# Reading the two halves of a matmul's moving operand in turn

## The chip, the cores and the metric

The kernel runs on one core of a Trainium2 chip. The metric is the device time of one execution in microseconds. Three runs of the kernel before gave 926.76, 927.38 and 1300.62 us; their median is 927.38 us.

## The reference

The inputs are `q`, `k`, `v` of shape 8 x 8 x 576 x 64 (batch, heads, sequence, head width) and three weight matrices. `k` and `v` are averaged over groups of 8 positions, so each head has 72 keys. Attention with softmax over these keys gives `x` of 4608 tokens x 512. A gated feed-forward block follows:

```python
gate = 1.0 / (1.0 + np.exp(-(x @ w_gate)))      # 4608x512 @ 512x1536
val = x @ w_val                                  # 4608x512 @ 512x1536
return (gate * val @ w_out).astype(np.float32)   # 4608x1536 @ 1536x512
```

Everything is float32. The three products of the feed-forward block (gate, value, output) are nearly all of the arithmetic.

## The kernel before, in words

The 4608 tokens are cut into 9 blocks of 512 (`BT`). Block 0 is done in a first pass (`first_pass`), with plain products. The other eight blocks are done as four pairs, and each of the three products of a pair is done with Strassen's seven products (numbered 1 to 7 as `m`) on halves of the matrices.

To keep float32 accuracy, each operand is split in two float32r parts, high and low (`split`), and each product is the sum of three matmuls: high x high, high x low, low x high. One TensorE matmul has a stationary operand of 128x128 (`lhsT`), which a weight load brings into the array, and a moving operand of 128 rows x 512 columns (`rhs`), which is streamed through it. The result, 128x512 float32, is summed up in a PSUM bank. In the names of the trace, `chain<-xo,parts` is a matmul of the gate and value products with `xo` (the activations, 512 tokens) moving and `parts` (weights) stationary, in `product` and `whole`. `acc<-hs,oparts` is a matmul of the output product in `second_sums`, with `hs` (the gated activations, 512 tokens) moving. `acc<-oparts,hs` is one of the output product of block 0 in `accumulate`, where the output weights `oparts` move (512 output columns) and `hs` is stationary.

In SBUF each moving operand is a contiguous run of 512 float32 words in each of the 128 partitions, and the matmul reads it from the first word to the last. Only the last step of the last pair splits one matmul group in a left and a right half of 256 columns.

Attention of the coming pair, the weight preparation (conversion of weights, the Strassen sums, splits), the activations and the stores run on DVE, ACT, POOL and the DMA queues beside the matmuls. The order of all instructions on every engine is fixed by hand: `ORDER` lists the work of the first pass word by word, `LATER` is a list of unit numbers for the four pairs. Line 320, on which the trace puts every instruction, is the one line through which recorded instructions are issued, so instructions are told apart by their tiles.

Block 0 leaves the kernel as rows (`out`, 512 tokens x 512), the other blocks transposed (`outT`, 512 x 4096), and the host puts both together.

Of the kernel before, what the change touches and what calls it, by code (L numbers as in the profile page):

```python
# [19 lines left out]
P = 128  # L20
# [6 lines left out]
DM, DF = 512, 1536  # L27
NC = DM // P
NF = DF // P
BT = 512  # L30
NB = B * S // BT
# [241 lines left out]
"""  # L273


class Taken:
# [56 lines left out]
def attention_then_ffn(ctx: ExitStack, tc: tile.TileContext, qT, kT, vm, vr, vn, sums8, wgv, wo, const, out, outT):  # L333
# [48 lines left out]
    words, parts, plain, oparts, wholes = {}, {}, {}, {}, {}  # L382
# [170 lines left out]
    def reload_s(m, q):  # L553

        t = otile([P, 2, 2, HALF], F32R, "oparts")
        if m < 4:
            half = slice(HALF, DM) if m == 3 else slice(0, HALF)
            for k in range(2):
                f = 4 * q + 2 * k + (m > 1)
                nc.sync.dma_start(t[:, k].bitcast(F32), kept_o[f][:, :, half].bitcast(F32))  # L560
        else:
            nc.sync.dma_start(t.rearrange("p k h n -> p k (h n)").bitcast(F32), kept_s[m, q].bitcast(F32))
        oparts[m, q] = t
# [254 lines left out]
    def product(kind, p, m):  # L818

        b = {1: "A", 6: "A", 7: "A", 4: "A", 2: "B", 5: "C", 3: "C"}[m]  # L820
        if m in (1, 2, 5):
            bank[kind, b] = ps.tile([P, BT], F32, name="chain", tag=CHAIN["GV".index(kind) * 3 + "ABC".index(b)])
        t, w, x = bank[kind, b], parts.pop((kind, p, m)), xo[m]
        with book.unit():
            for c in range(NC // 2):
                a = slice(c * P, (c + 1) * P)
                for k, (h, y) in enumerate(((0, 0), (0, 1), (1, 0))):
                    nc.tensor.matmul(
                        t, lhsT=w[:, h, a], rhs=x[:, y, c],
                        start=(m in (1, 2, 5) and c == 0 and k == 0), stop=(c == 1 and k == 2), skip_group_check=True,  # L830
                    )
        if m in (1, 5, 6):
            s = snap.tile([P, BT], F32, name=f"s{kind}{m}")
            nc.scalar.copy(s, t)
            seen[kind, m] = s
            return
        q = {2: (0, 0), 3: (0, 1), 7: (1, 1), 4: (1, 0)}[m]
        if m != 4:
            y = two.tile([P, BT], F32, name="y", tag="y")
            nc.vector.tensor_tensor(out=y, in0=t, in1=seen[kind, {2: 1, 3: 6, 7: 5}[m]], op=ALU.add)  # L840
        else:
            y = t
        if kind == "G":
            if m in (2, 7):
                gates[q[0]] = snap.tile([P, 2, BT], F32, name=f"gate{q[0]}")
            nc.scalar.activation(gates[q[0]][:, q[1]], y, AF.Sigmoid)
        else:
            f = 2 * p + q[1]
            nc.vector.tensor_tensor(
                out=hb[f // 4][:, f % 4, q[0] * BT:(q[0] + 1) * BT], in0=y, in1=gates[q[0]][:, q[1]], op=ALU.mult  # L850
            )
# [7 lines left out]
    def whole(kind, f, side, t=None):  # L859

        if t is None:
            t = ps.tile([P, BT], F32, name="chain", tag=CHAIN[turn[0] % 6])
            turn[0] += 1
        w = plain[kind, f]
        for c in range(NC):
            a = slice(c % 2 * P, c % 2 * P + P)
            x = xo[((1, 2), (5, 4))[side][c // 2]]
            with book.unit():
                for k, (h, y) in enumerate(((0, 0), (0, 1), (1, 0))):
                    nc.tensor.matmul(  # L870
                        t, lhsT=w[:, c // 2, h, a], rhs=x[:, y, c % 2],
                        start=(c == 0 and k == 0), stop=(c == NC - 1 and k == 2),
                    )
            yield t
# [139 lines left out]
    def second_sums(n, last, build, later):  # L1014
        A, B_, C = ("b4", "b5"), ("b0", "b3"), ("b1", "b2")
        acc, seen2 = {}, {}

        def result(side, half, c, bank, add):

            if add is None:  # L1020
                t = snap.tile([P, BT], F32, name="o", tag=f"sV{5 + c}")
            else:
                t = two.tile([P, BT], F32, name="o", tag="y")
            r, a = (half * 2 + c) * P, (2 * n - 2 + side) * BT
            if add is None and last and c:
                for k, copy in enumerate((nc.scalar.copy, nc.vector.tensor_copy)):
                    z = slice(k * BT // 2, (k + 1) * BT // 2)
                    copy(t[:, z], bank[:, z])
                    nc.sync.dma_start(outT[r:r + P, a + z.start:a + z.stop], t[:, z])
                return  # L1030
            if add is None:
                nc.scalar.copy(t, bank)
            else:
                nc.vector.tensor_tensor(out=t, in0=bank, in1=add, op=ALU.add)
            nc.sync.dma_start(outT[r:r + P, a:a + BT], t)

        units = [(m, q) for m in ((1, 5, 6, 2, 7, 3, 4) if last else (1, 5, 6, 2, 3, 7, 4)) for q in qs[n]]
        for u in units[:2]:
            reload_s(*u)
        for i, (m, q) in enumerate(units):  # L1040
            if i + 2 < len(units):
                reload_s(*units[i + 2])
            if i == 1:
                first_sums(qs[n][2])
            if i + 2 < len(units):
                operand(i + 2, *units[i + 2], n)
            hs = halves.pop((m, q))
            w = oparts.pop((m, q))
            name = {1: "A", 6: "A", 7: "A", 4: "A", 2: "B", 5: "C", 3: "C"}[m]
            cols, left, right = (slice(0, BT),), (slice(0, BT // 2),), (slice(BT // 2, BT),)  # L1050
            steps = ((0, (0, 1), cols), (1, (0, 1), cols))
            if last and i + 1 == len(units):
                steps = ((0, (0,), cols), (1, (0,), cols), (0, (1,), cols), (1, (1,), left), (1, (1,), right))
            for k, cs, (z,) in steps:
                with book.unit():
                    for c in cs:
                        if i % 3 == 0 and k == 0 and m in (1, 2, 5):
                            acc[name, c] = ps.tile([P, BT], F32, name="acc", tag={"A": A, "B": B_, "C": C}[name][c])
                        for t, (h, y) in enumerate(((0, 0), (0, 1), (1, 0))):
                            nc.tensor.matmul(  # L1060
                                acc[name, c][:, z], lhsT=w[:, k, h, c * P:(c + 1) * P], rhs=hs[:, y, k, z],
                                start=(m in (1, 2, 5) and i % 3 == 0 and k == 0 and t == 0), stop=(i % 3 == 2 and k == 1 and t == 2),
                                skip_group_check=True,
                            )
                if i == 0 and k == 1:
                    product("V", TURNS[n][-1], 4)
                    consumed("V", TURNS[n][-1], 4)
            if i % 3 == 2:
                for c in range(2):
                    t = acc[name, c]  # L1070
                    if m in (1, 5, 6):
                        s = snap.tile([P, BT], F32, name=f"s{'GV'[c]}{m}")
                        nc.scalar.copy(s, t)
                        seen2[m, c] = s
                    else:
                        side, half = {2: (0, 0), 3: (0, 1), 7: (1, 1), 4: (1, 0)}[m]
                        result(side, half, c, t, None if m == 4 else seen2[{2: 1, 3: 6, 7: 5}[m], c])
            if i in (8, 10, 12, 14, 19, 20):
                next(build, None)
        for _ in build:  # L1080
            pass
        for _ in range(3):
            next(later, None)
        s1.clear()
# [8 lines left out]
    def first_pass():  # L1093
# [46 lines left out]
        scs, rests, av, vp, raws, conv, ygate, vbank, hss, acc, outs, turned = ({} for _ in range(12))  # L1140
# [222 lines left out]
        def accumulate(f):  # L1363
            for i in range(QT):
                if f == 0:
                    acc[i] = bank_for([P, DM], "acc")
                a = slice(i * P, (i + 1) * P)
                for k, (y, w) in enumerate(((0, 0), (1, 0), (0, 1))):
                    nc.tensor.matmul(
                        acc[i], lhsT=hss[f // 2][:, y, f % 2, a], rhs=oparts[f // 2][:, f % 2, w],  # L1370
                        start=(f == 0 and k == 0), stop=(f == NF - 1 and k == 2),
                    )

# [90 lines left out]
```

## Time and profile before

| | |
|---|---|
| median of three runs | 927.38 us |
| span of the profiled execution | 924.9 us, 12542 instructions |
| PE (matmuls) busy | 914.2 us, 99% |
| PEld (weight loads) busy | 758.0 us, 82% |
| DVE busy | 694.2 us, 75% |
| ACT busy | 572.9 us, 62% |
| POOL busy | 24.1 us, 3% |
| DMA | 223.13 MB, mean 241 GB/s |
| granted TensorE clock | 0.998 of full speed, mean |

The profiled execution has no time of its own beside its span: the span is counted from the first to the last instruction, and the median of the runs shown is 2.5 us above it. PE and PEld are two rows for one engine, TensorE: weight loads run beside matmuls. Matmuls are pipelined, so the duration of one (about 390 ns for 512 columns) is longer than its share of the engine's time; the pace is read from the distance between the starts of matmuls that follow each other.

### The profile page before, as it was taken

The numbers are of one execution on the slowest core, as the hardware profiler recorded it, in microseconds if no ns is written. First come the engines' busy times: TensorE is split into PE (matmuls) and PEld (weight loads), VectorE is DVE, ScalarE is ACT, GpSimd is POOL, SyncE is SP. The second block draws the span as 40 slices with busy tenths as digits, with TensorE's granted clock in tenths as the row PEclk, the third lists the DMA queues.
The fourth block names the chain that finished last, engine by engine and source line by source line (L and its number), as shares of the span: only waits on it lengthen the run. The fifth ranks groups of instructions, "written<-read, shape, count | busy, mean of one in ns | idle before, by whom it ended". The sixth has DMA issues, their size and how long they took to land.

```text
span 924.9 us, 12542 instructions
## 1 busy us (share of the span) xinstructions
PE 914.2 (99%) x4375; PEld 758.0 (82%) x4375; DVE 694.2 (75%) x1062; ACT 572.9 (62%) x1044; POOL 24.1 (3%) x59
## 2 busy tenths in 40 slices
PE   8999999999999999999999999999999999999998
PEld 7778888888888888888888888888888888888886
DVE  6999978899999997886779966454668744444763
ACT  6999998689989665655466637343454443324442
POOL 1000000012120000000000000000000000000000
PEclk9999999999999999999999999999999999999999
DMA  9998786778989768897666676555556776555366
GB/s 332 378 359 323 281 308 248 274 238 297 327 301 329 256 193 261 291 308 231 211 216 223 198 236 229 180 166 178 181 174 196 229 223 222 176 193 182 97 208 197
DMA packets 90367, 223.13 MB, mean 241 GB/s; under 512 B 9536, under 2 KB 28480, under 8 KB 88768
## 3 DMA queue, kind: packets, MB, share of 16 engines
q1 hardware_dynamic: 85184, 203.97, 66.0%
q0 software_dynamic: 5120, 18.35, 5.0%
q8 instruction: 35, 0.57, 0.3%
q14 instruction: 28, 0.23, 0.1%
HBM read 168.81 MB, written 53.48 MB: 240 GB/s over the span
## 4 chain that ended last, share of the span: by engine, by line
PE 89%; ACT 5%; DVE 3%; DMA 1%; issue 1%; SPq 0%; DVEq 0%; ACTq 0%
PE chain L320 53%; PE acc L320 27%; PE av L320 4%; PE sc L320 4%; PE tp L320 2%; DMA early<-in_qT 1%; ACT L320 1%; DMA raw<-in_vr 1%; ACT parts L320 1%; ACT e L320 1%; SPq L320 0%; DVE early L320 0%; ACT early L320 0%; ACT raw L320 0%; DVE zs L320 0%
## 5 line engine op out<-in xcount | busy, mean ns | idle before, releaser
L320 PE MATMUL chain<-xo,parts 128*128 128x512 f32 x2316 | 559.7, 394 | 0.8 <-DVE y L320 0.8
L320 PEld LDWEIGHTS chain<-xo,parts 128*128 128x128 f32 x2316 | 427.5, 188 | 88.7 <-DVE y L320 1.4
L320 PE MATMUL acc<-hs,oparts 128*128 128x512 f32 x1011 | 235.3, 390 | 0.1
L320 PEld LDWEIGHTS acc<-hs,oparts 128*128 128x128 f32 x1011 | 188.2, 188 | 39.5 <-issue 1.0
L320 ACT CAST hs<-h 128x1024 fp32r<-128x1024 f32 x52 | 54.8, 1054 | 55.3 <-PE acc L320 48.0
L320 DVE TENSOR_TENSOR hs<-h,hs 128x1024 fp32r<-128x1024 f32 x52 | 63.4, 1221 | 32.4 <-ACT hs L320 32.4
L320 DVE TENSOR_TENSOR y<-chain,sV 128x512 f32<-128x512 f32 x69 | 47.3, 687 | 46.5 <-PE chain L320 28.2
L320 DVE TENSOR_TENSOR y<-chain,sG 128x512 f32<-128x512 f32 x69 | 47.1, 687 | 42.8 <-PE chain L320 25.6
L320 ACT COPY sV<-chain 128x512 f32<-128x512 f32 x69 | 40.3, 586 | 57.5 <-PE chain L320 50.1
L320 ACT ACTIVATE gate<-y 128x512 f32<-128x512 f32 x69 | 43.1, 632 | 43.7 <-DVE y L320 41.3
L320 ACT COPY sG<-chain 128x512 f32<-128x512 f32 x69 | 40.1, 587 | 47.1 <-PE chain L320 46.8
L320 ACT ACT_TABLE_LOAD x47 | 60.3, 1283 | 2.4 <-DVE m L320 1.3
L320 ACT CAST hs<-s 128x1024 fp32r<-128x1024 f32 x36 | 37.9, 1053 | 35.3 <-PE acc L320 23.8
L320 DVE TENSOR_TENSOR h<-y,gate 128x512 f32<-128x512 f32 x69 | 47.3, 689 | 2.0 <-ACT gate L320 0.4
L320 DVE TENSOR_TENSOR hs<-s,hs 128x1024 fp32r<-128x1024 f32 x36 | 43.9, 1220 | 4.4 <-ACT hs L320 4.3
L320 PE MATMUL sc<-kbd,raw 128*128 128x144 f32 (+1 forms) x260 | 41.1, 294 | 0.1
L320 PEld LDWEIGHTS sc<-kbd,raw 128*128 128x128 f32 (+1 forms) x260 | 34.3, 177 | 8.2 <-issue 2.6
L320 PE MATMUL acc<-oparts,hs 128*128 128x512 f32 x144 | 37.8, 398 | 0.0
L320 PEld LDWEIGHTS acc<-oparts,hs 128*128 128x128 f32 x144 | 26.4, 188 | 5.4 <-DVE early L320 0.2
L320 DVE TENSOR_TENSOR h<-h 128x256 f32<-128x256 f32 (+2 forms) x39 | 28.2, 727 | 2.0 <-DMA h<-keptwV 1.5
L320 DVE TENSOR_REDUCE m<-sc 128x4 f32<-128x288 f32 x48 | 21.7, 452 | 10.0 <-PE sc L320 9.7
L320 DVE TENSOR_TENSOR h<-chain,gate 128x512 f32<-128x512 f32 x23 | 15.8, 687 | 14.6 <-PE chain L320 14.6
(195 smaller groups left out, 1028.4 us busy)
## 6 DMA issues: line engine op xcount, KB each, us to landing
oparts<-keptS SPq DMA_DIRECT2D x48, 512.0 KB, 3.7
oparts<-keptO SPq DMA_DIRECT2D x72, 256.0 KB, 3.4
raw<-in_wgv SPq DMA_DIRECT2D x12, 1024.0 KB, 8.1
out<-o SPq DMA_DIRECT2D x35, 256.0 KB, 4.5
raw<-in_kT SPq DMA_DIRECT2D x28, 288.0 KB, 4.8
raw<-in_qT SPq DMA_DIRECT2D x29, 256.0 KB, 4.3
raw_o<-in_wo SPq DMA_DIRECT2D x12, 512.0 KB, 6.3
keptO<-oparts SPq DMA_DIRECT2D x12, 512.0 KB, 4.0
```

The source lines that it names most:

```text
L320: return self._book.take(lambda: f(*args, **named))
```

## The change

A helper `by_halves` turns a run of 512 words into the order 0, 256, 1, 257, 2, 258 and so on. The matmuls of the three products read their moving operand in that order. The number of matmuls, their columns, their stationary operands and their destinations in PSUM are the same; the result's columns come out in the turned order. For the gate and value products the columns are tokens, so `h` and `hs` hold tokens in turned order, and the output product of the pairs turns them a second time. In block 0 the tokens are turned once (by the first two products) and the output columns once (by the third). The host puts rows and columns back in place after the device is done. Matmuls of the attention part, transposes and weight loads are as before.

```diff
+def by_halves(x):
+
+    return x.rearrange("p (i j) -> p j i", i=2)
@@ product
-                        t, lhsT=w[:, h, a], rhs=x[:, y, c],
+                        t, lhsT=w[:, h, a], rhs=by_halves(x[:, y, c]),
@@ whole
-                        t, lhsT=w[:, c // 2, h, a], rhs=x[:, y, c % 2],
+                        t, lhsT=w[:, c // 2, h, a], rhs=by_halves(x[:, y, c % 2]),
@@ second_sums
-                                acc[name, c][:, z], lhsT=w[:, k, h, c * P:(c + 1) * P], rhs=hs[:, y, k, z],
+                                acc[name, c][:, z], lhsT=w[:, k, h, c * P:(c + 1) * P],
+                                rhs=by_halves(hs[:, y, k])[:, z.start // 2:z.stop // 2],
@@ accumulate
-                        acc[i], lhsT=hss[f // 2][:, y, f % 2, a], rhs=oparts[f // 2][:, f % 2, w],
+                        acc[i], lhsT=hss[f // 2][:, y, f % 2, a], rhs=by_halves(oparts[f // 2][:, f % 2, w]),
@@ kernel, on the host
-    return np.concatenate([r.results[0]["out_0"], r.results[0]["out_1"].T], axis=0)
+    turned = np.arange(BT).reshape(2, BT // 2).T.reshape(-1)
+    first, rest = np.empty((BT, DM), f32), np.empty((NB - 1, BT, DM), f32)
+    first[turned[:, None], turned] = r.results[0]["out_0"]
+    rest[:, turned[turned]] = r.results[0]["out_1"].T.reshape(NB - 1, BT, DM)
+    return np.concatenate([first, rest.reshape(-1, DM)], axis=0)
```

## Rows read from the trace of the kernel before

**Rows 1.** The page, span and busy time: busy us, share of the span, instructions.

```profile
span 924.9 us, 12542 instructions
...
PE 914.2 (99%) x4375; PEld 758.0 (82%) x4375; DVE 694.2 (75%) x1062; ACT 572.9 (62%) x1044; POOL 24.1 (3%) x59
```

**Rows 2.** The page, the chain of work that ended last, shares by engine.

```profile
PE 89%; ACT 5%; DVE 3%; DMA 1%; issue 1%; SPq 0%; DVEq 0%; ACTq 0%
```

**Rows 3.** Groups by line with shapes kept apart, matmuls: count | busy us, mean ns.

```profile
L320 PE MATMUL chain<-xo,parts 128*128 128x512 f32 x2316 | 559.7, 394 | 0.8 <-DVE y L320 0.8
L320 PE MATMUL acc<-hs,oparts 128*128 128x512 f32 x1005 | 234.8, 391 | 0.1
L320 PE MATMUL acc<-oparts,hs 128*128 128x512 f32 x144 | 37.8, 398 | 0.0
...
L320 PE MATMUL acc<-hs,oparts 128*128 128x256 f32 x6 | 0.9, 282 | 0.0
```

**Rows 4.** Timeline of PE, 700 to 800 us: start, us, instructions merged with their count.

```profile
700.27 27.36 PE L320 MATMUL acc<-hs,oparts 128*128 128x512 f32 x120
727.47 1.52 PE L320 MATMUL chain<-xo,parts 128*128 128x512 f32 x6
728.83 11.04 PE L320 MATMUL acc<-hs,oparts 128*128 128x512 f32 x48
```

**Rows 5.** Timeline of PE, 20 to 23 us: the sums of `v` in block 0.

```profile
21.44 1.46 PE L320 MATMUL vp<-early,xs 128*128 128x256 f32 x6
22.74 0.59 PE L320 MATMUL vp<-xs 128*128 128x256 f32 x2
```

**Rows 6.** Timeline of PE, 281 to 290 us: attention matmuls among those of the products.

```profile
282.54 0.28 PE L320 MATMUL av<-ph,vh 128*128 128x256 f32 x1
...
282.90 0.28 PE L320 MATMUL av<-pr,vres 96*128 96x256 f32 x1
283.02 2.91 PE L320 MATMUL chain<-xo,parts 128*128 128x512 f32 x12
285.77 0.65 PE L320 MATMUL sc<-kbd,raw 128*128 128x144 f32 x4
```

**Rows 7.** Busy time by stage: us, busy of PE, PEld, DVE, ACT, POOL; clock; DMA.

```profile
0.00:100.00 100.00, 93.99 (x500) 78.45 (x501) 88.13 (x154) 89.83 (x204) 2.49 (x19) 0.98 0.92 338
...
200.00:300.00 100.00, 99.24 (x492) 82.33 (x491) 96.52 (x181) 89.45 (x190) 16.67 (x31) 1.00 0.86 308
300.00:400.00 100.00, 100.00 (x488) 82.25 (x487) 90.39 (x137) 63.31 (x111) 0.55 (x1) 1.00 0.78 252
...
700.00:800.00 100.00, 100.00 (x442) 82.78 (x442) 59.74 (x64) 42.31 (x56) 0.00 (x0) 1.00 0.67 212
```

**Rows 8.** Groups by line with shapes kept apart, 0 to 100 us.

```profile
L320 PE MATMUL chain<-xo,parts 128*128 128x512 f32 x183 | 46.4, 398 | 0.0
L320 PE MATMUL acc<-oparts,hs 128*128 128x512 f32 x48 | 12.9, 400 | 0.0
```

**Rows 9.** Groups by line with shapes kept apart, 200 to 300 us.

```profile
L320 PE MATMUL chain<-xo,parts 128*128 128x512 f32 x348 | 85.7, 397 | 0.8 <-DVE y L320 0.8
...
L320 PE MATMUL acc<-hs,oparts 128*128 128x512 f32 x18 | 4.2, 389 | 0.0
```

## The prediction

> **What bounds the kernel now.** I read the page first: TensorE's matmuls are busy 914.2 of 924.9 us [rows 1], and the chain that ended last is 89% PE [rows 2]. Busy time of pipelined matmuls says little, so the next view is the groups by shape: 2316 + 1005 + 144 = 3465 matmuls of the three products with 512 columns, and 6 with 256 [rows 3]. Those are the instructions that the diff touches. Third, the timeline gives their pace from start to start, and this is the number on which everything rests: 120 of them start between 700.27 and 727.47 us, which is 27.20 / 120 = 226.7 ns each [rows 4]. 3465 x 226.7 = 786 us, so 85% of the span is this one pace. [...] Whatever changes the pace changes the time nearly one for one; whatever does not is hidden.
>
> **Where the pace comes from.** [...] In the sums of `v`, 6 matmuls of 256 columns take 22.74 - 21.44 = 1.30 us, 216 ns each [rows 5]. [...] Second, the pace is not fixed even for one shape: right after attention matmuls, 12 of the same kind take 285.77 - 283.02 = 2.75 us, 229 ns each, with no change in columns [rows 6]. [...]
>
> **The change, part by part.**
>
> The host's reordering lies outside the device time: 0. The number of matmuls, weight loads, PSUM writes, copies, DMAs and waits is unchanged; no step is moved past a queue, and no wait is added. DVE and ACT work on permuted columns at the same shapes and strides: 0, with nothing that has to cover it. [...]
>
> What is left is the price of a 512-column matmul whose moving words come alternately from two places 1024 bytes apart. No row of this trace has a moving operand read that way. [...]
>
> I take 216 ns. [...] Gain: 226.7 - 216 = 10.7 ns x 3465 = 37.1 us.
>
> [...]
>
> What of the 37.1 us does not arrive? **The first 100 us** hold 183 + 48 = 231 of the matmuls [rows 8], worth 2.5 us, while the DMA share is 0.92 and the PE is only 93.99 us busy [rows 7]: loads set part of that stage. I count half, 1.2 us lost. **From 200 to 300 us** there are 348 + 18 = 366 [rows 9], worth 3.9 us, and DVE is busy 96.52 of 100 us [rows 7]; it can give at most 3.5 us, and not all of its idle time is in the right place. I count 2 us lost there; from 300 to 400 us DVE has 9.6 us free, and ACT 10.6 us or more in both stages, so what is late next is DVE's conversion and Strassen work of the second stage, and no other. The loss in the slower matmuls after attention work I leave as it is. Sum: 924.9 - 37.1 + 1.2 + 2 = 891.0 us of span; the runs' median stands 2.5 us above the span, so 893.5, say 893 us.
>
> This case's own range: at 213.3 ns everywhere, with nothing lost to DVE or DMA and some 3 us back from the unsettled stretches, 927.4 - 46.4 - 3 = 878, and with a little more 876; with only half of the lost steps recovered, 221.3 ns, 927.4 - 18.7 = 909.
>
> [...]
>
> [...]
>
> [...]
>
> [...]
>
> **How the numbers follow.** Forecast 0.62, no change 0.18, an access per word 0.16, more collisions 0.04. The predicted time is the forecast's, 893 us. About 2% is what a measurement of this kernel can tell from no change, 909 to 946 us. The forecast's own range is 876 to 909; to hold 8 in 10 the range takes in the no-change case, up to 940, and leaves out the two slow ones. Faster by over 2%: the forecast without its weak end, 0.60. Within 2%: no change with that end, 0.20. Slower: 0.20.
>
> **What would show it.** In the timeline from 700 to 800 us, the starts of the matmuls should be 216 ns apart, with the clock at 1.00 as before: that alone proves or refutes the pace. [...] In the stages table, PE's share should stay near 100 late, and fall a little between 200 and 300 us, with DVE above 97; new waits of `chain` for DVE tiles there would be the 2 us. If the pace falls to 216 and the time does not, the gain went to those waits. [...]

## The result, and the profile after

The changed kernel takes 903.81 us (median of 4 runs, 903.00 to 904.84) against 926.76 us (median of 3): a ratio of 0.9754, 95% interval 0.9739 to 0.9768. It is faster by 2.5%, 10.8 us above the forecast of 893 us and inside the range. The execution at 1300.62 us among the runs of the kernel before is a disturbed one and is left out of the median and the ratio. (The traces after call the issuing line 325, for 320 before, because five lines were added above it.)

The page of the changed kernel, span and busy time, to be read beside [rows 1]:

```profile
span 901.2 us, 12542 instructions
...
PE 881.0 (98%) x4375; PEld 759.8 (84%) x4375; DVE 695.6 (77%) x1062; ACT 579.6 (64%) x1044; POOL 24.1 (3%) x59
```

The instructions are the same. PE is busy 33.2 us less, but the span is shorter by 23.7 us only. ACT, with the same work, is busy 6.7 us longer: that is the first sign that something beside the pace has changed.

The timeline of PE in the changed kernel (start, us, instructions merged). The first two rows answer to [rows 4], the others to [rows 6]:

```profile
685.40 26.06 PE L325 MATMUL acc<-hs,oparts 128*128 128x512 f32 x120
711.30 1.52 PE L325 MATMUL chain<-xo,parts 128*128 128x512 f32 x6
...
286.00 2.76 PE L325 MATMUL chain<-xo,parts 128*128 128x512 f32 x12
288.59 0.65 PE L325 MATMUL sc<-kbd,raw 128*128 128x144 f32 x4
```

(711.30 - 685.40) / 120 = 215.8 ns, where it was 226.7. And the 12 matmuls right after attention, which took 229 ns each before, take 2.59 / 12 = 215.8 ns too: the unsettled stretches are gone. Over all distances below 260 ns from one 512-column matmul to the next instruction, the mean fell from 228.1 ns (3336 of them) to 215.9 ns (3304): 12.2 ns x 3465 = 42.2 us. Of these, 23.7 us reached the span. So the question is where some 18 us went.

Two views answer it. First, the rows of the output product's matmuls, where the last two figures of time are the starts of the first and of the last instruction; kernel before, then changed kernel:

```profile
L320 PE MATMUL acc<-hs,oparts x1011: 278/389/498, 296.1 to 920.8; 128*128 128x512 f32 x168, 128*128 128x256 f32 x1
L320 PE MATMUL acc<-oparts,hs x144: 387/389/497, 63.0 to 175.5; 128*128 128x512 f32 x144
```

```profile
L325 PE MATMUL acc<-hs,oparts x1011: 273/379/483, 298.8 to 896.1; 128*128 128x512 f32 x168, 128*128 128x256 f32 x1
L325 PE MATMUL acc<-oparts,hs x144: 377/379/483, 65.0 to 181.0; 128*128 128x512 f32 x144
```

The last matmul of block 0 starts at 181.0 us instead of 175.5: the changed kernel is 5.5 us *behind* there. It is 2.7 us behind at the first output product of the pairs (298.8 against 296.1), and 24.7 us ahead at the end. With 498, 444 and 2523 of the matmuls in these three stretches, 12.2 ns each would have given 6.1, 5.4 and 30.8 us. What came was -5.5, 2.8 and 27.4: 11.6 us are missing in the first stretch, 2.6 and 3.4 in the other two, 17.5 us in all with rounding. (The first figure is a little too low. The profiled execution of the kernel before had a mean granted clock of 0.66 from 10 to 15 us, where the changed kernel's was 1.00, and its first matmul of the products started at 32.4 us instead of 31.0. Counted from there, the changed kernel is 6.9 us behind at the end of block 0.)

Second, the two ACT operations and the DVE operation that convert 64-bit weights (minimum/median/maximum ns, first and last start); they read every second word of `raw`. Kernel before, then changed kernel:

```profile
L320 ACT ACTIVATE w<-raw x12: 1131/1151/1211, 16.3 to 119.5; 128x1024 f32<-128x1024 f32 x12
L320 ACT ACTIVATE raw<-raw,cst x12: 1219/1258/1329, 17.3 to 120.5; 128x1024 uint32<-128x1024 uint16 x12
L320 DVE SCALAR_TENSOR_TENSOR w<-w,raw x12: 1211/1218/1228, 21.7 to 121.8; 128x1024 uint32<-128x1024 uint32 x12
```

```profile
L325 ACT ACTIVATE w<-raw x12: 1143/1370/1556, 14.9 to 124.4; 128x1024 f32<-128x1024 f32 x12
L325 ACT ACTIVATE raw<-raw,cst x12: 1215/1545/1738, 15.9 to 125.5; 128x1024 uint32<-128x1024 uint16 x12
L325 DVE SCALAR_TENSOR_TENSOR w<-w,raw x12: 1216/1439/1660, 20.3 to 127.2; 128x1024 uint32<-128x1024 uint32 x12
```

They became 18 to 23% longer in the median, with nearly the same minimum: only some of them are hit. The timeline tells which. Two of the `w<-raw` in the changed kernel (start, us):

```profile
25.71 1.14 ACT L325 ACTIVATE w<-raw 128x1024 f32<-128x1024 f32 x1
57.12 1.56 ACT L325 ACTIVATE w<-raw 128x1024 f32<-128x1024 f32 x1
```

The first ran before any matmul of the products, the second in the middle of 18 of them. Of the 12, the three beside which no such matmul ran took 1143 to 1204 ns, and the four that had one beside them for over 90% of their time took 1539 to 1556 ns. The casts `hs<-h` on ACT, 128x1024, which read their words in a row, are not hit: 1054 ns before and 1048 after, in the mean. The changed kernel's busy time by stage (columns as in [rows 7]) and PE's waits from 100 to 180 us (who waited for whom; us in total, times, longest):

```profile
0.00:100.00 100.00, 92.02 (x488) 75.96 (x489) 87.83 (x149) 92.03 (x197) 2.49 (x19) 1.00 0.90 331
...
200.00:300.00 100.00, 98.20 (x504) 83.88 (x503) 98.29 (x189) 89.97 (x193) 17.21 (x32) 1.00 0.87 314
...
700.00:800.00 100.00, 100.00 (x465) 87.27 (x464) 52.53 (x63) 39.06 (x56) 0.00 (x0) 1.00 0.69 219
```

```profile
PE acc L325 <- ACT oparts L325: 1.2, 2, 0.7
PE chain L325 <- ACT y L325: 0.9, 1, 0.9
PE sc L325 <- DVE pl L325: 0.7, 1, 0.7
PE tp L325 <- ACT y L325: 0.7, 1, 0.7
```

In the first 100 us PE starts 488 matmuls instead of 500, and ACT is at 92%. From 100 to 180 us PE waits for ACT's `oparts` and `y`; before the change no wait for ACT shows in the first 180 us. From 700 us on, PE is full and 465 matmuls start instead of 442.

### The profile page after: what moved, and what is told of

The parts are those of the page before. It is cut to its first block, busy times and chain, and to the rows that moved or that the text cites. A ratio compares the mean times of both kernels' runs of the same rounds, so it can differ in the third digit from the quotient of the medians.

```text
span 901.2 us, 12542 instructions
## 1 busy us (share of the span) xinstructions
PE 881.0 (98%) x4375; PEld 759.8 (84%) x4375; DVE 695.6 (77%) x1062; ACT 579.6 (64%) x1044; POOL 24.1 (3%) x59
## 4 chain that ended last, share of the span: by engine, by line
PE 68%; DVE 5%; ACT 5%; issue 3%; DMA 2%; POOL 1%; POOLq 0%; DVEq 0%; ACTq 0%
PE chain L325 40%; PE acc L325 22%; PE av L325 3%; PE sc L325 2%; ACT L325 1%; PE tp L325 1%; DMA keptV0C<-parts 1%; DVE hs L325 1%; DVE s L325 1%; DMA oparts<-keptS 1%; DVE xo L325 1%; ACT hs L325 1%; DVE h L325 1%; ACT gate L325 1%; ACT e L325 0%
## 5 line engine op out<-in xcount | busy, mean ns | idle before, releaser
L325 PE MATMUL chain<-xo,parts 128*128 128x512 f32 x2316 | 532.2, 383 | 3.6 <-ACT y L325 1.1
L325 PE MATMUL acc<-hs,oparts 128*128 128x512 f32 x1011 | 224.1, 380 | 0.9 <-DMA oparts<-keptS 0.9
L325 ACT CAST hs<-h 128x1024 fp32r<-128x1024 f32 x52 | 54.5, 1048 | 47.7 <-PE acc L325 40.6
L325 DVE TENSOR_TENSOR hs<-s,hs 128x1024 fp32r<-128x1024 f32 x36 | 43.8, 1218 | 3.9 <-ACT hs L325 3.9
L325 DVE TENSOR_REDUCE zs<-e 128x16 f32<-128x1152 f32 x15 | 20.2, 1349 | 6.3 <-ACT e L325 6.3
```

The costliest lines, as they stand in the source:

```text
L325: return self._book.take(lambda: f(*args, **named))
```

## The experiments

**Where the loss sits: only the pairs, only block 0.** In the first, `whole` reads by halves only where the pairs call it, and `accumulate` reads as before; in the second, only those two places of block 0 read by halves.

```diff
 e1_pairs_only
-  rhs=by_halves(x[:, y, c % 2])                  # whole, when called for block 0
+  rhs=x[:, y, c % 2]
-  rhs=by_halves(oparts[f // 2][:, f % 2, w])     # accumulate
+  rhs=oparts[f // 2][:, f % 2, w]
 e2_first_only
-  by_halves(...) in product, second_sums, and in whole when called for the pairs
+  contiguous there
```

> The products of block 0 in the first pass read their moving operand contiguously again; only the four pairs read by halves. Theory A (collision): the alternating reads slow those ACT and DVE operations of the weight conversion that read every second word, and the first pass, which ACT feeds, loses more than the pace gives. Then here the conversion's two activations are back at about 1257 and 1151 ns (changed kernel: 1545 and 1370), the first pass ends as before the change, near 175 us instead of 181, and the whole takes 896 to 900 us. Theory B (the first pass is simply fed by others, and the slower conversion is a coincidence of that run): conversions stay slow or fast independently of this edit, the first pass ends no earlier than in the changed kernel, and the whole takes 903 to 907 us.

> The counterpart: only the products of block 0 read by halves, the four pairs contiguously. Theory A: conversions slow (about 1545 and 1370 ns), the first pass ends near 181 us, and the whole is slower than before the change: 930 to 934 us, although 432 of its matmuls have a pace of 216 instead of 227 ns. Theory B: not slower than before, 922 to 928 us.

Measured: pairs only 896.33 us (ratio to before 0.9671, interval 0.9651 to 0.9691); block 0 only 934.01 us (1.0083, 1.0066 to 1.0100), slower than the kernel before. The conversions and the end of block 0, pairs only and then block 0 only:

```profile
L325 ACT ACTIVATE w<-raw x12: 1122/1140/1220, 15.3 to 118.8; 128x1024 f32<-128x1024 f32 x12
L325 ACT ACTIVATE raw<-raw,cst x12: 1216/1244/1329, 16.3 to 119.8; 128x1024 uint32<-128x1024 uint16 x12
...
L325 PE MATMUL acc<-oparts,hs x144: 387/389/497, 62.3 to 174.0; 128*128 128x512 f32 x144
```

```profile
L325 ACT ACTIVATE w<-raw x12: 1121/1358/1563, 14.7 to 124.5; 128x1024 f32<-128x1024 f32 x12
L325 ACT ACTIVATE raw<-raw,cst x12: 1227/1584/1793, 15.8 to 125.6; 128x1024 uint32<-128x1024 uint16 x12
...
L325 PE MATMUL acc<-oparts,hs x144: 377/379/483, 65.0 to 181.9; 128*128 128x512 f32 x144
```

Both fit theory A and neither fits B. With block 0 read by halves, the conversions' medians are 1358 and 1584 ns instead of 1140 and 1244, and the last matmul of block 0, which ACT feeds, starts 6 to 8 us later (181.0 and 181.9 us, for 175.5 and 174.0 with contiguous reads there), although the pace of its own matmuls is 216 ns.

**What makes 216 ns: runs of two and of four words.** Still from the two halves in turn, but in runs (the host's order is adapted, here and below).

```diff
 e3_two_words:  x.rearrange("p (i j) -> p j i", i=2)  ->  x.rearrange("p (i j t) -> p j i t", i=2, t=2)
 e5_four_words: x.rearrange("p (i j) -> p j i", i=2)  ->  x.rearrange("p (i j t) -> p j i t", i=2, t=4)
```

> As the changed kernel, but two neighbouring words are read from the left half, then two from the right. If the two streams give the pace by taking turns at all (theory C), it stays at 216 ns; if the turn must come with every word (theory D), it lies between 216 and 227 ns. Under theory A with the number of separate places per word as what collides, the conversion's first activation lies between 1257 and 1545 ns and the whole takes 893 to 902 us with theory C; with theory D 905 to 925 us.

> As the changed kernel, but four neighbouring words (16 bytes) are read from each half in turn. Theory C: pace 216 ns. Theory D: 227 ns, as contiguous. Theory A: no more separate places per word than a contiguous read of 16-byte pieces, so the conversion's activations are at 1257 and 1151 ns as before; with the pace of theory C the whole takes 888 to 896 us, with that of D 924 to 930 us.

Both theories failed. Two words at a time took 1281.78 us (1.3837, 1.3816 to 1.3857), four 1004.17 us (1.0838, 1.0821 to 1.0855), slower than contiguous. The same 120 matmuls in the timeline, for two and for four words:

```profile
952.07 40.17 PE L325 MATMUL acc<-hs,oparts 128*128 128x512 f32 x120
992.07 2.17 PE L325 MATMUL chain<-xo,parts 128*128 128x512 f32 x6
```

```profile
755.01 30.16 PE L325 MATMUL acc<-hs,oparts 128*128 128x512 f32 x120
785.01 1.67 PE L325 MATMUL chain<-xo,parts 128*128 128x512 f32 x6
```

That is 333 and 250 ns (the median over all such matmuls is 254 for four words). The second activation of the conversion, for two and for four words:

```profile
L325 ACT ACTIVATE raw<-raw,cst x12: 1219/1266/1377, 16.1 to 147.0; 128x1024 uint32<-128x1024 uint16 x12
```

```profile
L325 ACT ACTIVATE raw<-raw,cst x12: 1224/1662/1756, 16.5 to 127.9; 128x1024 uint32<-128x1024 uint16 x12
```

That PE's reads and the conversions collide stands (1662 ns beside runs of four words, 1258 beside contiguous reads), but theory A's reason for it, the number of separate places per word, fell. With four words the two activations had medians of 1662 and 1458 ns, at least as slow as by halves, though a run of four is read from one place. With two words they had 1266 and 1158 ns, hardly longer than before the change.

**Two lanes.** These paces suggest theory L: words go in turn to two lanes, and what counts is how often a lane finds its next word in the piece of four words (16 bytes) that it has. The two lanes and the size of the piece are the author's assumption; no run shows either by itself. Counted in this way, by halves one lane walks through the left half and the other through the right, four words to a piece (216 ns); with contiguous reading each lane has two words of a piece (227 ns), with runs of two only one (333 ns). Four orders test it, two far apart, two that keep the two lanes but bring them close together.

```diff
 e4_even_odd:   x.rearrange("p (j i) -> p i j", i=2)           # 0, 2, 4, ... then 1, 3, 5, ...
 e7_quarters:   x.rearrange("p (i j) -> p j i", i=4)           # 0, 128, 256, 384, 1, ...
 e6_near_eight: x.rearrange("p (g i j) -> p g j i", i=2, j=8)  # 0, 8, 1, 9, ... in each 16
 e8_near_four:  x.rearrange("p (g i j) -> p g j i", i=2, j=4)  # 0, 4, 1, 5, ... in each 8
```

> As the changed kernel, but the order is all even words, then all odd words: one stream with a step of two words. Theory L (two lanes, formed on the runs of two and four words): words go alternately to two lanes, each lane keeps the 16-byte piece that it read last, and the pace is set by how many of a lane's words in a row lie in one piece: 4 give 216 ns (by halves), 2 give 227 (contiguous) to 254 (four words in turn), 1 gives 333 (two words in turn). Here each lane takes every fourth word, one per piece: 300 ns or more. Rival M (what costs is that neighbours in time are neighbours in memory): 216 ns.

> As the changed kernel, but word by word from four quarters in turn (two dimensions, as by halves). Theory L: each lane alternates between two quarters, one word of a piece at a time: 300 ns or more. Rivals M and N: 216 ns.

> As the changed kernel, but the two streams are 8 words apart instead of 256: inside each 16 words the order is 0, 8, 1, 9, ... 7, 15. Theory L: each lane has 4 words in a row of each piece, 216 ns. Rival N (a pattern with three dimensions costs time at each carry, which would also explain the runs of two and four words): 230 ns or more. Rival D (the distance of half a tile matters): 227 ns or more. For the conversion operations: if they collide with the two streams' distance, they come back to about 1257 and 1151 ns, and the whole takes 888 to 898 us; if they collide with any turn between pieces, they stay near 1545 and 1370 and the whole is 901 to 907 us.

> As the changed kernel, but inside each 8 words the order is 0, 4, 1, 5, 2, 6, 3, 7: one lane reads one 16-byte piece, the other lane the next. Theory L: 4 words in a row of each piece, 216 ns. Rival N: 230 ns or more. The conversion operations as in the run with 8 words: back to 1257 and 1151 ns if the distance matters (888 to 898 us in all), near 1545 and 1370 if not (901 to 907 us).

The timelines of even then odd words and of quarters (one run each), and of the order with 4 words, each with the same 120 matmuls:

```profile
1253.37 54.31 PE L325 MATMUL acc<-hs,oparts 128*128 128x512 f32 x120
1307.51 2.89 PE L325 MATMUL chain<-xo,parts 128*128 128x512 f32 x6
```

```profile
828.95 34.17 PE L325 MATMUL acc<-hs,oparts 128*128 128x512 f32 x120
862.95 1.87 PE L325 MATMUL chain<-xo,parts 128*128 128x512 f32 x6
```

```profile
675.63 26.06 PE L325 MATMUL acc<-hs,oparts 128*128 128x512 f32 x120
701.53 1.50 PE L325 MATMUL chain<-xo,parts 128*128 128x512 f32 x6
```

| order | words in a row per lane and 16 bytes | ns per matmul | run, us |
|---|---|---|---|
| halves; 8 apart; 4 apart | 4 | 216 | 904; 894; 893 |
| contiguous | 2 | 227 | 927 |
| four words in turn | 2 | 250 | 1004 |
| quarters | 1 | 283 | 1110 |
| two words in turn | 1 | 333 | 1282 |
| even, then odd | 1 | 451 | 1698 |

The ranking is that of theory L, and the three rivals fall: M and N by the quarters and by even and odd words (216 ns expected by one or both, 283 and 451 measured) and N and D by the two near orders (a pattern of three dimensions, streams 16 and 32 bytes apart, 216 ns). Among orders with the same count L doesn't give the sizes (283 to 451 ns for a count of 1), and its 300 ns for the quarters was too much. It is a model that ranks the orders that were run, not a structure that was shown.

The near orders also give the faster kernel: 894.07 us with 8 words (0.9646, 0.9627 to 0.9664) and 892.76 us with 4 (0.9637, 0.9622 to 0.9653). In the kernel with 4 words the conversions and the two landmarks are:

```profile
L325 ACT ACTIVATE w<-raw x12: 1126/1149/1212, 14.9 to 117.1; 128x1024 f32<-128x1024 f32 x12
L325 ACT ACTIVATE raw<-raw,cst x12: 1208/1254/1287, 16.0 to 118.1; 128x1024 uint32<-128x1024 uint16 x12
...
L325 PE MATMUL acc<-hs,oparts x1011: 272/379/483, 288.5 to 886.5; 128*128 128x512 f32 x168, 128*128 128x256 f32 x1
L325 PE MATMUL acc<-oparts,hs x144: 377/379/483, 61.6 to 171.0; 128*128 128x512 f32 x144
```

The pace is that of the changed kernel (215.8 ns), the conversions are as before the change (1149 and 1254 ns, for 1151 and 1258), and block 0 ends at 171.0 us: 10.0 us earlier than in the changed kernel and 4.5 us earlier than before. The whole difference between 904 and 893 us lies in block 0 (at the end, 886.5 against 896.1 us). So with the collision removed, 4.5 of the 6.1 us that the pace is worth in the first stretch arrive, 1.4 us of them already before the first matmul of the products (31.0 us against 32.4, see above).

**From which distance the streams collide.** The same order with the streams 128, 64 and 32 words apart (`j=128`, `j=64`, `j=32`), one run each.

> As the run with 4 words, but the two streams are 128 words (512 bytes) apart, inside each 256 words. The pace is 216 ns by theory L. Theory P (the collision comes only where the two streams are a certain distance apart, such as 1024 bytes and not 512): conversions at about 1257 and 1151 ns, 891 to 897 us. Theory Q (it grows with the distance): between those values and the 1545 and 1370 ns of the changed kernel, 896 to 903 us.

> The two streams are 64 words (256 bytes) apart. Pace 216 ns. Theory P: conversions at about 1257 and 1151 ns, 891 to 897 us. Theory Q: a little slower than that, less than with 128 words.

> The two streams are 32 words (128 bytes) apart. Pace 216 ns. Both theories: conversions within 3% of 1257 and 1151 ns, 891 to 897 us.

The pace was 216 ns in all three (25.90 us for the same 120 matmuls in each). The second activation of the conversion at 128, 64 and 32 words (the first had medians of 1368, 1377 and 1166 ns):

```profile
L325 ACT ACTIVATE raw<-raw,cst x12: 1217/1558/1806, 16.0 to 125.9; 128x1024 uint32<-128x1024 uint16 x12
```

```profile
L325 ACT ACTIVATE raw<-raw,cst x12: 1227/1582/1787, 15.6 to 125.3; 128x1024 uint32<-128x1024 uint16 x12
```

```profile
L325 ACT ACTIVATE raw<-raw,cst x12: 1218/1282/1313, 15.9 to 118.9; 128x1024 uint32<-128x1024 uint16 x12
```

Times: 906.40, 906.18 and 895.40 us. Both P and Q fell. In these three runs it is neither one special distance nor a slope but a step between 128 bytes (1282 ns, within 2% of the 1258 of the kernel before) and 256 bytes (1582 ns, with 1558 at 512 and 1545 at 1024).

**What still holds the matmuls up from 180 to 330 us.** The sums of keys and values are cut short, on top of the order with 4 words.

```diff
 e12_less_dve
-        pool(ks, load("k", b, p), nc.vector)
+        pool(ks, load("k", b, p)[:, :, :2], nc.vector)     # and the two of the values alike
```

> The order with 4 words, and in the attention of blocks 3 to 8 the sums of keys and values over 8 positions read only the first 2 of them, so that DVE has some 0.5 us less work in each of about 45 of its operations; that part of the output is not computed. If what still keeps the matmuls waiting between 180 and 330 us is DVE (theory R), most of the 5 us that they lose there come back: 886 to 890 us, with DVE under 146 of 150 us busy in that stage. If it is something else (theory S: transfers or ACT), the time stays at 892 to 894 us.

Measured: 892.95 us (0.9633, 0.9616 to 0.9651), no change against 892.76. The stage 180 to 330 us in the kernel with 4 words, and in this one, then PE's longest wait there in this one:

```profile
180.00:330.00 150.00, 147.78 (x751) 126.42 (x750) 148.08 (x257) 127.84 (x267) 19.37 (x36) 1.00 0.83 289
```

```profile
180.00:330.00 150.00, 147.31 (x751) 126.53 (x750) 142.33 (x257) 127.83 (x267) 19.30 (x36) 1.00 0.84 289
```

```profile
PE chain L325 <- DVE y L325: 1.7, 2, 1.6
```

DVE has 5.8 us less to do and PE starts the same 751 matmuls. Theory R falls: DVE is nearly full there in the kernel with 4 words (148.08 of 150 us), but its total is not what PE waits for. The longest wait that remains is for single results (`y`; 0.6 us in the kernel with 4 words). A likely reason is that the chain of operations which makes them after a matmul is as long as before, but that was not shown, and nothing that shortens it was tried.

The trace narrows the place down. In the kernel with 4 words, from the end of block 0 to the first output product of the pairs, the distances from one matmul of the products to the next sum up to 93.9 us instead of 98.8, as the pace has it. The 168 distances into, within and out of the groups of attention matmuls grew from 21.9 to 23.7 us. So nearly all that is lost in that stretch is lost at the attention matmuls. Why stays open, and so do the 6.4 us in all that are missing after block 0 in that kernel.

## Why the prediction was right, and where it was off

*The pace.* The number is right, 215.8 ns for a forecast of 216, and the gain came from the read, since the order of the read is all that changed for these matmuls. But no row of the kernel before shows 216 ns for a matmul of 512 columns: [rows 5] has it for 256 columns, `sum_v` issues 8 of those matmuls into `vp`, and the trace has 16 records about 216 ns apart, so how often one of their words is read is not shown. The 216 ns were the author's estimate, and that they fit this order so closely was in part luck. Taking turns between two places is not enough, either: the halves and the near orders run at 216 ns, but runs of two words, which take turns between the halves as well, at 333, and the quarters at 283. Among the orders that were run, 216 ns came only with a turn at every word between two streams. No run shows the 213.3 ns of the range's fast end, nor the lost steps of which its weak end recovers half; the shortest pace measured over the 120 matmuls was 215.8 ns, in the changed kernel and in each of the orders with two streams 4 to 128 words apart.

*The slower matmuls after attention.* Left as they were in the sum; they are gone (229 ns before, 215.8 after), and the pace is worth 42.2 us instead of 37.1. What made them slow is not shown: in the kernel before, a weight load starts 2 to 4 ns after the start of nearly every matmul of the products, in the steady stretches and in the slower ones, and no run moved the loads.

*DVE and ACT, "0, with nothing that has to cover it".* This is the step of the sum that failed. The shapes and strides of their operations were the same, but not their durations: the conversions read every second word at the same time as PE's two distant streams, and grew by 18 to 36% in the medians (`raw_o<-raw_o,cst` from 1242 to 1603 ns). By the medians this is 12 x (0.29 + 0.22) + 6 x (0.36 + 0.42) = 10.8 us of ACT (9.9 us when the 36 operations are added up one by one), spread from 15 to 149 us, where ACT had 10 us free in the first 100.

*What does not arrive: 3.2 us.* Measured 42.2 - 24.7 = 17.5 us to the start of the last matmul. Of it, 10.0 us are the collision: by so much block 0 ends earlier in the kernel with 4 words. That kernel's 892.8 us are the forecast's 893, but not because the other terms held. The pace was worth 5.1 us more than forecast, and 42.2 - 34.3 = 7.9 us of it did not reach the span (924.9 to 890.6 us) instead of 3.2; the two errors cancel. For 200 to 300 us the forecast gave 2 us and DVE as the reason. The rows agreed (PE 98.20, DVE 98.29), the reason did not: less DVE work brought nothing.

*The rivals.* No change, an access for each word and more collisions did not come: the pace went from 226.7 to 215.8 ns, and that of the 12 matmuls after attention from 229 to 215.8. Nor do the runs show that words that follow each other have to lie close together: by halves they are 1024 bytes apart (216 ns), in the order of even and odd words 8 bytes (451 ns).

## What to carry to other kernels

The steady pace of a saturated engine is worth a question of its own, even when the engine is "busy" 99% of the span (914.2 of 924.9 us here); the order in which a float32r moving operand is read is worth 5% per matmul (226.7 to 215.8 ns) and costs no instruction. Take the order that is close together (word by word from two runs 4 or 8 words apart): it gave all of the pace (215.8 ns), and no other operation that was compared grew: with 4 words ACT is busy 569.1 us and DVE 690.7, for 572.9 and 694.2 before. When an edit changes how one engine reads SBUF, compare the durations of every other engine's operations before and after, strided ones first; equal shapes were no proof of equal times here (1258 and 1545 ns).

## What the hardware showed that was not expected

A matmul's moving read slowed operations of ACT and DVE. An activation that reads and writes every second word went from 1258 to 1545 ns, and a DVE operation that reads every second word from 1218 to 1439 (medians), beside matmuls that take words in turn from two streams 1024 bytes apart. The activation did so at 512 and 256 bytes too (1558 and 1582 ns), and not at 128, 32 and 16 bytes (1282, 1248 and 1254). Contiguous casts stayed (`hs<-h`, 1055 and 1048 ns).

Distance alone does not decide it. Beside runs of two words from the two halves (1266 ns) and quarters (1254 ns) the activation stayed, and in both PE itself took 283 ns or more for a matmul. Beside runs of four words from the two halves (250 ns) it took 1662 ns. What sets this, and why the step lies between 128 and 256 bytes, was not tried.

A contiguous read was not the fastest order for a float32r moving operand: 227 ns against 216, and with a step of two words a matmul took 451 ns, about twice as long.
